# Filter rows in halves, later k-v products and paired value tiles in a fused attention and long-convolution kernel

## The chip, the cores and the metric

The kernel runs on one core of one Trainium2 chip. Its time is the device time of one execution in microseconds. The core has five engines that run their own instruction streams and wait for one another through semaphores: TensorE (PE, with the weight loads shown as PEld), VectorE (DVE), ScalarE (ACT), GpSimd (POOL) and SyncE (SP). SP, ACT and POOL issue DMA transfers, which run on 16 DMA engines.

## The reference

Two independent branches are computed in bf16 and laid side by side in the output (2048 x 1024).

- A: attention over x (2048 x 512) with 32 heads of width 16. `qkv = x @ wqkv`, softmax of `q k^T / 4` over all 2048 keys (no mask), times v, heads joined, `@ wo`.
- B: a gated long convolution over 512 channels. k is shifted and weighted by four taps, `kv = k_shift * v`, then every channel d is convolved causally with its own filter `ssm_k[d]` of length 2048 (the reference does it by FFT), `kv * ssm_D` is added, and the result is multiplied by q.

## The kernel before

*Attention.* Scores are made transposed, in blocks of 128 keys x 512 queries of one head: four query blocks, eight groups of four heads, 16 key tiles, 2048 blocks. The blocks are walked in 695 steps (`chunks`), of three blocks each, or of two in every second step of the first 56 (`N_EARLY`) and at the end. In a step PE makes the scores (L453) into one of two sets of three PSUM banks, ACT takes the exponential of the whole set in one instruction (L460), and two steps later PE multiplies by V (L525). Of each group, four blocks have their exponential computed on DVE instead (L478 to L494). Since the scores use two bank sets, PE can be one step ahead of ACT.

*Convolution.* Channel d's filter is written reversed and zero-padded to a scratch in HBM (`kz_scratch`); loading it with a step of one element from partition to partition gives a 128 x 2048 Toeplitz row `WR[:, r, :]`, 512 KB. There are 12 places r for such rows. Places 5 to 9 first hold k turned (`KTR`), from which the product of k and v is made, so they come free only when a block of 128 channels (c = 0 to 3) has its four products. A quad `qd` is four channels; its convolution is 16 lags of four small matmuls each (`conv_lags`, L648). Lag n uses columns 128 (15 - n) to 128 (16 - n) of the row, so lags 0 to 7 read the second half of a row and lags 8 to 15 the first. Two quads share PSUM bank 7, after which DVE evicts (L662); after eight quads a turn, a product with q and, after eight turns, stores follow.

*Order.* The instruction lists of all engines are written by one loop over the steps T: scores, products with V, then `emit_bg`, which puts at most one piece of background work into the step. The background jobs are the projections of q, k and v (L285, L292, L299), the products of k and v (`prod_job`, L341, evicted at L353), the output projection (L594) and the convolution. Each job has a due step and an earliest step in `todo`; a job is cut into pieces of about half a PSUM bank's matmuls. Before step 56 jobs use bank 5, later bank 7. `st["time"]` is a budget: each step adds 0.42, 0.74 or 0.78 and each piece takes 0.47. The lags are spread evenly up to step `CONV_END`, at most five a step.

*Loads.* `load_wr` issues filter rows on SP, in the order of the channels, as soon as a place is named free; SP waits for the last matmul of the row that was there. SP's queue is in order, so a load that waits holds all that follow, the loads of q and the stores of B among them. `land` is the planner's own estimate of when a row will be there, 1.33 us a row; `conv_ready` lets lags be placed only from that step on. On the chip PE waits for the real load, and the scores that follow wait behind it in PE's queue. Three other queues are touched by the change: DVE's pieces `kv_pieces` (copies of q's weights, turning of the filter), the filler matmuls `warm`, and `keep_busy_end`.

Of the kernel before, what the change touches and what calls it, by code (L numbers as in the profile page):

```python
# [37 lines left out]
CONV_END = 668  # L38
# [57 lines left out]
def bass_concat_heads__mha_block__ssm_conv_h3__prompt_kernel(  # L96
# [89 lines left out]
    d_wr = [DmaSem(sem(f"d_wr{i}")) for i in range(R_W)]  # L186
# [34 lines left out]
    h_w0 = dve.op(lambda e: e.memset(PT[:, 0, 0:512], 0.0))  # L221
# [55 lines left out]
    def pe_unit(u, bank, dcs=(0, 1, 2, 3)):  # L277
# [9 lines left out]
        elif kind == "k":  # L287
# [6 lines left out]
        else:  # L294
            _, kt, z = u
            deps += h_x[kt // 4] + [h_wv]

            def mm(e, dc):
                return e.matmul(PS[:, bank, 0:256], lhsT=xT[:, dc, kt * 128:(kt + 1) * 128],  # L299
                                rhs=WV[:, dc, 256 * z:256 * z + 256], start=(dc == 0), stop=(dc == 3))  # L300

# [7 lines left out]
    def evac_unit(u, bank, h, eng=None):  # L309
        kind = u[0]  # L310
        if kind == "q":
            _, qb, g = u
            hh = dve.op(lambda e: e.tensor_scalar(QT[:, qb % 2, g, :], PS[:, bank, :], QSCALE, None, ALU.mult),  # L313
                        [h])
            h_q[(qb, g)] = hh
        elif kind == "k":
# [7 lines left out]
        else:  # L324
            _, kt, z = u
            dst = VAF[:, kt, 0:H * VW].rearrange("p (h e) -> p h e", e=VW)[:, 16 * z:16 * z + 16, 0:DH]
            src = PS[:, bank, 0:256].rearrange("p (h e) -> p h e", h=16)
            hh = dve.op(lambda e: e.tensor_copy(dst, src), [h, h_vaf1])  # L328
            h_v[(kt, z)] = hh
        bank_free[bank] = hh  # L330

# [44 lines left out]
    def warm(e):  # L376
        ins = None
        for _ in range(12):
            ins = e.matmul(PS[:, 0, :], lhsT=PT[:, 0, 0:128], rhs=PT[:, 0, 0:512], start=True, stop=True)
        return ins  # L380
    pe.op(warm, [h_w0])
# [161 lines left out]
    def finish_group(n, h, T):  # L543
# [8 lines left out]
        assert n < 4 or len(h_prod) == 16  # L552
# [145 lines left out]
    def unit_job(*u):  # L698
        def job(T, bank):
            if u[0] == "v":  # L700
                return [lambda: unit(u, bank)]
# [3 lines left out]
    def prod_job(c, j):  # L705
        def job(T, bank):
            def last():
                prod_out(c, j, bank, prod_mm(c, j, 2, 4, bank))
                if sum(k[0] == c for k in h_prod) == 4:
                    slots.extend((r, h_prod_mm[c]) for r in ((5,), (6,), (7,), (8, 9))[c])  # L710
# [23 lines left out]
    todo = [(when(0, 0, kt) + 1, x_at[kt // 4], 1, unit_job("v", kt, 0)) for kt in range(KT)]  # L734
    todo += [(when(0, 4, kt) + 1, 0, 1, unit_job("v", kt, 1)) for kt in range(KT)]
    todo += [(when(0, 2 * o, 4 * sc), x_at[sc], 2, unit_job("k", o, sc)) for o in range(4) for sc in range(4) if o or sc]
# [205 lines left out]
```

## Time and profile before

| | |
|---|---|
| median of 3 runs | 925.04 us (923.96 to 927.89) |
| the profiled execution | 928.67 us |
| its span | 926.7 us |
| granted TensorE clock, mean | 0.987 |
| ACT busy | 892.0 us, 96% |
| PE busy | 771.5 us, 83% |
| DVE busy | 637.7 us, 69% |
| DMA moved | 289.36 MB, mean 312 GB/s |

The span goes from the first to the last instruction; the time of the execution has some 2 us around it. A busy share is an average over all stages. In a group of instructions, `128x1536` is partitions by elements, the number after `x` the count; the idle time in front of a group has the name of the engine and line that ended it. In the windows, a row gives the stretch, its length, the busy time of PE, PEld, DVE, ACT and POOL with their instructions, the clock, the share of the DMA engines and GB/s. In the DMA rows, "under 512 B" and so on count packets by size. The code numbers the steps from 0; the exponential of step T is the T-th row of L460.

### The profile page before, as it was taken

The page shows a single profiled execution, that of the slowest core. Times are in us where ns is not written, and L with a number is a line of the kernel's source. Part 1 is how long each engine was busy: PE and PEld are TensorE (multiplying, and loading weights), DVE is VectorE, ACT ScalarE, POOL GpSimd, SP SyncE. Part 2 cuts the span into 40 slices and gives each one's busy share as a digit, 9 for nine tenths or more (in the row PEclk, how much of TensorE's full clock was granted, in tenths as well). Part 3 has the DMA queues.
Part 4 walks back from the last instruction along what each step waited for, and adds up shares of the span by engine and source line. Part 5 has one row for each costly group of instructions (what it writes and reads, how often), then busy time and mean ns, then how long its engine had stood idle before and what let it go on. Part 6 is the DMA issues. An engine that isn't in the chain of part 4 may idle for free.

```text
span 926.7 us, 29497 instructions
## 1 busy us (share of the span) xinstructions
PE 771.5 (83%) x13428; PEld 354.6 (38%) x13482; DVE 637.7 (69%) x817; ACT 892.0 (96%) x701; POOL 22.2 (2%) x38
## 2 busy tenths in 40 slices
PE   7998888888788878888888788888888888877887
PEld 2333433333334333334334334333334443444422
DVE  3426678778677676777777767686777777667674
ACT  4999999999999999999999989999999999999997
POOL 3000000003000000000000000000000000000000
PEclk8999999999999999999999989999999999999999
DMA  9970741889999999999999999999999999999810
GB/s 246 257 253 31 242 139 46 318 294 296 405 370 371 353 370 337 374 326 379 378 373 378 346 391 364 335 379 364 386 382 379 328 364 356 403 397 376 334 47 23
DMA packets 105035, 289.36 MB, mean 312 GB/s; under 512 B 25680, under 2 KB 38480, under 8 KB 104528
## 3 DMA queue, kind: packets, MB, share of 16 engines
q1 hardware_dynamic: 101680, 284.33, 84.8%
q8 instruction: 106, 1.74, 0.7%
q0 software_dynamic: 832, 2.10, 0.7%
q10 hardware_dynamic: 2400, 1.05, 0.5%
q14 instruction: 17, 0.14, 0.0%
HBM read 277.35 MB, written 6.42 MB: 306 GB/s over the span
## 4 chain that ended last, share of the span: by engine, by line
ACT 69%; PE 15%; DVE 8%; DMA 5%; issue 1%; SPq 1%; ACTq 0%; POOL 0%; DVEq 0%
ACT PT L460 69%; PE PS L453 4%; DMA WR<-kz_scratch 4%; PE PS L525 4%; DVE EH L489 2%; PE PS L341 2%; PE PS L299 2%; PE PS L594 2%; PE PS L292 1%; PE PS L648 1%; DVE KV L353 1%; DVE KTo L322 1%; DMA SHK<-in_B_shift_k_dram 1%; SPq L173 1%; DVE PTD L494 1%
## 5 line engine op out<-in xcount | busy, mean ns | idle before, releaser
L460 ACT ACTIVATE PT<-PS 128x1536 bf16<-128x1536 f32 (+1 forms) x695 | 888.0, 1572 | 21.4 <-PE PS L453 20.6
L453 PE MATMUL PS<-QT,KTo 32*128 32x512 bf16 x2048 | 275.0, 389 | 105.9 <-ACT PT L460 94.0
L648 PE MATMUL PS<-WR,KV 128*11 128x128 bf16 (+15 forms) x8192 | 295.2, 224 | 18.5 <-DMA WR<-kz_scratch 9.2
L525 PE MATMUL PS<-PT,VAF 128*32 128x512 bf16 x1928 | 292.4, 393 | 1.3 <-DVE VAF L328 1.0
L648 PEld LDWEIGHTS PS<-WR,KV 128*9 128x9 bf16 (+15 forms) x8192 | 191.9, 107 | 61.1 <-issue 41.3
L453 PEld LDWEIGHTS PS<-QT,KTo 32*128 32x128 bf16 x2048 | 67.7, 91 | 257.7 <-ACT PT L460 210.5
L489 DVE SCALAR_TENSOR_TENSOR EH<-EH,EM 128x1024 f32<-128x1024 f32 x120 | 151.7, 1264 | 3.4
L478 DVE TENSOR_SCALAR EI<-PS 128x512 int32<-128x512 f32 x120 | 85.0, 708 | 72.1 <-PE PS L453 70.7
L525 PEld LDWEIGHTS PS<-PT,VAF 128*32 128x32 bf16 x1928 | 69.0, 93 | 148.1 <-issue 138.8
L489 DVE SCALAR_TENSOR_TENSOR EH<-EM 128x1024 f32<-128x1024 f32 x60 | 77.2, 1287 | 0.0
L494 DVE SCALAR_TENSOR_TENSOR PTD<-EH,EI 128x1024 bf16<-128x1024 f32 x60 | 74.5, 1241 | 1.7
L546 DVE STREAM_TRANSPOSE DT<-PS 128x512 f32<-128x512 f32 x31 | 22.9, 739 | 60.0 <-PE PS L525 57.0
L662 DVE CAST YB<-PS 128x256 bf16<-128x256 f32 x64 | 26.8, 419 | 27.5 <-PE PS L525 13.8
L482 DVE TENSOR_SCALAR EM<-EI 128x1024 int32<-128x1024 int32 x60 | 44.4, 739 | 1.7
L484 DVE TENSOR_SCALAR EI<-EI 128x1024 int32<-128x1024 int32 x60 | 42.8, 714 | 2.1
L313 DVE TENSOR_SCALAR QT<-PS 128x512 bf16<-128x512 f32 x32 | 22.1, 690 | 26.1 <-PE PS L285 26.1
L285 PE MATMUL PS<-xT,WQP 128*128 128x512 bf16 x101 | 32.3, 382 | 6.5 <-issue 3.0
L594 PE MATMUL PS<-WKV,OTN 128*128 128x512 bf16 x114 | 33.2, 382 | 4.4 <-issue 1.6
L525 PE MATMUL PS<-PTD,VAF 128*32 128x512 bf16 x120 | 24.0, 397 | 1.3 <-DVE PTD L494 1.2
L773 PE MATMUL PS<-IDN,ZR 128*16 128x128 bf16 x308 | 24.8, 222 | 0.2 <-issue 0.2
L328 DVE CAST VAF<-PS 128x256 bf16<-128x256 f32 x32 | 13.5, 421 | 16.3 <-PE PS L299 16.2
L563 DVE STREAM_TRANSPOSE OTN<-OB 128x512 bf16<-128x512 bf16 (+1 forms) x33 | 23.7, 717 | 0.7
(61 smaller groups left out, 252.9 us busy)
## 6 DMA issues: line engine op xcount, KB each, us to landing
WR<-kz_scratch SPq DMA_DIRECT2D x512, 512.0 KB, 7.9
kz_scratch<-WR SPq DMA_DIRECT2D x1, 2176.0 KB, 12.6
QN<-in_B_q_dram SPq DMA_DIRECT2D x8, 256.0 KB, 8.8
out_dram<-KV SPq DMA_DIRECT2D x16, 128.0 KB, 2.9
out_dram<-OUTA POOLq DMA_DIRECT2D x12, 128.0 KB, 5.2
QT<-in_B_ssm_k_dram SPq DMA_DIRECT2D x1, 1024.0 KB, 5.6
QN<-in_B_ssm_k_dram SPq DMA_DIRECT2D x1, 1024.0 KB, 7.6
OTN<-in_B_v_dram SPq DMA_DIRECT2D x1, 1024.0 KB, 6.5
```

Source lines behind the costliest of these rows:

```text
L285: return e.matmul(PS[:, bank, :], lhsT=WQP[:, dc, g, :], rhs=xT[:, dc, qb * 512:(qb + 1) * 512], start=(dc == 0), stop=(dc == 3))
L453: ins = e.matmul(PS[:, bank, :], lhsT=KTo[32 * s:32 * s + 32, g // 2, kt * 128:(kt + 1) * 128], rhs=QT[32 * s:32 * s + 32, qb % 2, g, :], ...
L460: h_exp[T] = act.op(lambda e: e.activation(PT[:, T % R_PT, 0:n * QB], PS[:, banks[0]:banks[0] + n, :].rearrange("p b f -> p (b f)"), ACT.E ...
L478: h_fix[i] = dve.op(lambda e: e.tensor_scalar(EI[:, i % 2, :], PS[:, bank, :], FIX_LO, FIX_ADD, ALU.max, ALU.add), [h, h_pair.get(p - 1)])
L482: st["m"] = dve.op(lambda e: e.tensor_scalar(EM[:, :, :], EI[:, :, :], 0x7fffff, 0x3f800000, ALU.bitwise_and, ALU.bitwise_or), [h_fix[i], ...
L484: st["e"] = dve.op(lambda e: e.tensor_scalar(EI[:, :, :], EI[:, :, :], 0x7f800000, 0x40000000, ALU.bitwise_and, ALU.bitwise_xor), [st["m"]])
L489: st["h"] = dve.op(lambda e: e.scalar_tensor_tensor(EH[:, :, :], src, (B3, B2, B1)[j], m, ALU.add, ALU.mult), [st["m"], st.get("h")])
L494: lambda e: e.scalar_tensor_tensor(PTD[:, :, :], EH[:, :, :], B0, EI[:, :, :].bitcast(FP32), ALU.add, ALU.mult), [st["h"], st["e"], h_ptd. ...
L525: ins = e.matmul(PS[32 * s:32 * s + 32, pvb(qb * NG + g), :], lhsT=VAF[:, kt, h * VW:h * VW + 32], rhs=rhs, start=(kt == 0), stop=(kt == K ...
L594: ins = e.matmul(PS[:, bank, :], lhsT=OTN[:, oslot(qb * NG + g), t * 128:(t + 1) * 128], rhs=WOP[:, g, :], start=(g == 0), stop=(g == NG - 1))
L648: ins = e.matmul(PS[32 * c:32 * c + NB - n, BGB, col:col + 128], lhsT=KV[:, n:NB, d], rhs=WR[:, slot_of[d], 128 * (NB - 1 - n):128 * (NB - ...
L662: bank_free[BGB] = h_yb[qd // 8] = dve.op(lambda e: e.tensor_copy(dst, src), [h, h_turn.get(qd // 8 - 1)])
```

## The change

- Each filter row is loaded as two halves of 256 KB, with a place and a semaphore of its own for each (24 in all). The second half (z = 1) is loaded ahead of the first for four rows at a time. A half's place is free again after the last lag that reads it. Lags 0 to 7 wait for the second halves alone. The planner books 0.67 us a half.
- The products of k and v for channel block 0 are due at steps 50 to 53 (before 40 to 43). Those of blocks 1 to 3 are due at 88 to 152, mixed, where they were due at 54 to 87. The places they hold come free accordingly.
- The value projections are made in pairs of key tiles: two tiles' matmuls go into one bank and one DVE instruction evicts both. Only the first two tiles stay single.
- In the first 56 steps the budget adds 0.45 a step and a piece takes 0.55. Projections of k and q are due four steps earlier; q of the second query block is allowed from step 140 or 156 (before 92).
- DVE's `kv_pieces` run in steps 4 to 6 and after 10 (before 0 to 2 and after 10). Three filler matmuls are added in step 0.
- `CONV_END` is 674 (before 668); the end filler is left out in steps in which bank 7 was evicted.

```diff
-CONV_END = 668
+CONV_END = 674
...
-    d_wr = [DmaSem(sem(f"d_wr{i}")) for i in range(R_W)]
+    d_wr = [DmaSem(sem(f"d_wr{i}")) for i in range(2 * R_W)]
...
+    def v_mm(kt, z, i, bank):
+        def fn(e):
+            ins = None
+            for dc in range(4):
+                ins = e.matmul(PS[:, bank, 256 * i:256 * i + 256], lhsT=xT[:, dc, (kt + i) * 128:(kt + i + 1) * 128],
+                               rhs=WV[:, dc, 256 * z:256 * z + 256], start=(dc == 0), stop=(dc == 3))
+            return ins
+        return pe.op(fn, h_x[kt // 4] + [h_wv, bank_free[bank] if i == 0 else None])
+
+    def v_out(kt, z, n, bank, h):
+        dst = VAF[:, kt:kt + n, 0:H * VW].rearrange("p t (h e) -> p t h e", e=VW)[:, :, 16 * z:16 * z + 16, 0:DH]
+        src = PS[:, bank, 0:256 * n].rearrange("p (t h e) -> p t h e", t=n, e=DH)
+        bank_free[bank] = hh = dve.op(lambda e: e.tensor_copy(dst, src), [h, h_vaf1])
...
-    pe.op(warm, [h_w0])
+    pe.op(lambda e: warm(e, 12, 0), [h_w0])
...
-    slots = [(r, None) for r in (0, 1, 2, 3, 4, 10, 11)]
+    slots = {z: [(r, None) for r in (0, 1, 2, 3, 4, 10, 11)] for z in range(2)}
     slot_of, land = {}, {}
+    next_row = [0, 0]
     def load_wr(T):
-        while slots and len(slot_of) < C:
-            d = len(slot_of)
-            r, h = slots.pop(0)
-            src = bass.AP(tensor=kz_ap.tensor, offset=kz_ap[d, 0].offset, ap=[[1, 128], [1, S]])
-            h_wr[d] = dma(sp, d_wr[r], WR[:, r, :], src, [h_kzw[0], h])
-            slot_of[d] = r
-            st["dma"] = max(st["dma"], now(T) + 2.5) + 1.33
-            land[d] = st["dma"] + 1.0
+        while True:
+            z = 1 if next_row[1] // 4 == next_row[0] // 4 and next_row[1] % 4 >= next_row[0] % 4 and next_row[0] % 4 == 0 else 0
+            d = next_row[z]
+            if d == C or not slots[z]:
+                return
+            next_row[z] += 1
+            r, h = slots[z].pop(0)
+            src = bass.AP(tensor=kz_ap.tensor, offset=kz_ap[d, 1024 * z].offset, ap=[[1, 128], [1, 1024]])
+            h_wr[(d, z)] = dma(sp, d_wr[2 * r + z], WR[:, r, 1024 * z:1024 * z + 1024], src, [h_kzw[0], h])
+            slot_of[(d, z)] = r
+            st["dma"] = max(st["dma"], now(T) + 2.5) + 0.67
+            land[(d, z)] = st["dma"] + 1.0
...
-        deps = [h_wr[4 * qd + c] for c in range(4)] + [h_prod[(4 * qd // 128, j)] for j in range(4)]
+        deps = [h_wr[(4 * qd + c, z)] for c in range(4) for z in ([1] if n0 < 8 else []) + ([0] if n1 > 8 else [])] + [h_prod[(4 * qd // 128, j)] for j in range(4)]
...
-                                   rhs=WR[:, slot_of[d], 128 * (NB - 1 - n):128 * (NB - n)],
+                                   rhs=WR[:, slot_of[(d, 1 - n // 8)], 128 * (NB - 1 - n):128 * (NB - n)],
...
         h = pe.op(fn, deps)
+        for z in range(2):
+            if n0 < (NB, 8)[z] <= n1:
+                slots[z].extend((slot_of[(4 * qd + c, z)], h) for c in range(4))
+        load_wr(T)
         if n1 == NB:
-            slots.extend((slot_of[4 * qd + c], h) for c in range(4))
-            load_wr(T)
...
-    todo = [(when(0, 0, kt) + 1, x_at[kt // 4], 1, unit_job("v", kt, 0)) for kt in range(KT)]
-    todo += [(when(0, 4, kt) + 1, 0, 1, unit_job("v", kt, 1)) for kt in range(KT)]
+    todo = [(when(0, 0, kt) + 1, x_at[kt // 4], n, unit_job("v", kt, 0, n)) for kt, n in [(0, 1), (1, 1)] + [(i, 2) for i in range(2, KT, 2)]]
+    todo += [(when(0, 4, kt) + 1, 0, 2, unit_job("v", kt, 1, 2)) for kt in range(0, KT, 2)]
...
-    todo += [((40, 54, 70, 84)[c] + j, max(18 + 2 * c, 24 if j >= 2 else 0), 2, prod_job(c, j))
+    todo += [(((50, 51, 52, 53), (88, 100, 106, 112), (94, 118, 124, 146), (100, 134, 140, 152))[c][j], max(18 + 2 * c, 24 if j >= 2 else 0), 2, prod_job(c, j))
              for c in range(4) for j in range(4)]
...
-        return (T >= N_EARLY and d < C and land.get(d + 3, 1e9) <= now(T)
+        return (T >= N_EARLY and d < C and land.get((d + 3, 1 - st["lag"] // 8), 1e9) <= now(T)
...
             unit(("q", 0, 1), 5)
+            pe.op(lambda e: warm(e, 3, 7), [bank_free[7]])
...
-        st["time"] = min(st["time"] + (0.78 if T >= N_EARLY else 0.42 if T % 2 else 0.74), 1.1)
+        st["time"] = min(st["time"] + (0.78 if T >= N_EARLY else 0.45), 1.1)
...
-                st["time"] -= 0.47
+                st["time"] -= 0.47 if T >= N_EARLY else 0.55
...
+            if n0 < 8 < n1 and land.get((4 * st["qd"] + 3, 0), 1e9) > now(T):
+                n1 = 8
...
-        elif st["qd"] == C // 4 and T < NT - 14:
+        elif st["qd"] == C // 4 and T < NT - 14 and bank_free[BGB] is st["seen"]:
             keep_busy_end(T)
...
-        if kv_pieces and (T < 3 or T > 10):
+        if kv_pieces and (4 <= T < 7 or T > 10):
```

More of the change, by code (lines that the diff above doesn't have):

```diff
@@ L312, in evac_unit @@
             _, qb, g = u
+            assert qb != 1 or all((c, 2 + g // 4) in h_prod for c in range(4))
             hh = dve.op(lambda e: e.tensor_scalar(QT[:, qb % 2, g, :], PS[:, bank, :], QSCALE, None, ALU.mult),
@@ L323, in evac_unit @@
             h_k[(o, sc)] = hh
[L324 to L329, printed above, removed]
-        bank_free[bank] = hh
+        bank_free[bank] = hh
+    def v_mm(kt, z, i, bank):
[10 more added lines that the diff above has]
+        bank_free[bank] = hh = dve.op(lambda e: e.tensor_copy(dst, src), [h, h_vaf1])
+        for i in range(n):
+            h_v[(kt + i, z)] = hh
     def unit(u, bank, eng=None):
@@ L550, in finish_group @@
         ob = OB[:, :].rearrange("p (b i) -> p b i", i=32)
-        assert n < 4 or len(h_prod) == 16
+        assert not 4 <= n < 12 or all((c, n // 4 - 1) in h_prod for c in range(4))
         def scale():
@@ L787, in emit_bg, with bg_step @@
     def emit_bg(T):
+        bg_step(T)
+        st["seen"] = bank_free[BGB]
+    def bg_step(T):
         if not st["wop"] and len(h_v) == 2 * KT and len(h_k) == 16:
@@ L807, in emit_bg @@
             jobs = bg_jobs(T)
-            if jobs and (st["gap"] or not conv_ready(T) or urgent(T, jobs)):
+            if jobs and (st["gap"] or T >= N_EARLY and not conv_ready(T) or urgent(T, jobs)):
                 j = jobs[0]
```

31 lines of the change are left out of this document (14 added, 17 removed).

## The prediction

> **What bounds the kernel now.** I read the page's engine totals first, then the ACT waits, then ACT's stages in windows, then the DMA rows.
>
> ```profile
> span 926.7 us, 29497 instructions
> PE 771.5 (83%) x13428; PEld 354.6 (38%) x13482; DVE 637.7 (69%) x817; ACT 892.0 (96%) x701; POOL 22.2 (2%) x38
> L460 ACT ACTIVATE PT<-PS 128x1536 bf16<-128x1536 f32 (+1 forms) x695 | 888.0, 1572 | 21.4 <-PE PS L453 20.6
> 24.00:86.00 62.00, 58.27 (x494) 24.60 (x498) 24.18 (x44) 57.28 (x50) 0.00 (x0) 1.00 0.67 198
> 86.00:161.00 75.00, 64.57 (x810) 27.81 (x817) 58.44 (x83) 71.84 (x56) 0.00 (x0) 1.00 0.40 134
> ```
>
> ScalarE is the bound: 695 exponentials fill 888.0 of 926.7 us, and the change leaves all 695 (the same blocks, the same 120 on VectorE). Only ACT's holes can move. Its holes between exponentials are 20.6 us, nearly all waits for the scores matmul. In the last two rows (columns: window, length, busy time of PE, PEld, DVE, ACT, POOL, clock, DMA share, GB/s) ACT lacks 62.00 - 57.28 = 4.7 us and 75.00 - 71.84 = 3.2 us, with PE at 94% and 86%.
>
> ```profile
> 15.98 1.02 ACT L460 ACTIVATE PT<-PS 128x1024 bf16<-128x1024 f32 x1 [0.99 <-PE PS L453]
> 18.04 1.45 ACT L460 ACTIVATE PT<-PS 128x1536 bf16<-128x1536 f32 x1 [1.03 <-PE PS L453]
> ...
> 22.14 2.37 ACT L460 ACTIVATE PT<-PS 128x1536 bf16<-128x1536 f32 x2 [1.03 <-PE PS L453]
> ...
> 44.42 2.41 ACT L460 ACTIVATE PT<-PS 128x1536 bf16<-128x1536 f32 x2 [0.18 <-PE PS L453]
> 47.01 2.37 ACT L460 ACTIVATE PT<-PS 128x1536 bf16<-128x1536 f32 x2 [0.18 <-PE PS L453]
> ...
> 52.22 4.74 ACT L460 ACTIVATE PT<-PS 128x1536 bf16<-128x1536 f32 x4 [0.23 <-PE PS L453]
> ...
> 241.50 2.80 ACT L460 ACTIVATE PT<-PS 128x1536 bf16<-128x1536 f32 x2 [1.21 <-PE PS L453]
> ...
> 535.51 1.47 ACT L460 ACTIVATE PT<-PS 128x1536 bf16<-128x1536 f32 x1 [2.25 <-PE PS L453]
> ```
>
> Three kinds of hole are seen. At 16 to 22 us steps lose about 1 us each. Around 45 us a pair of steps takes 47.01 - 44.42 = 2.59 us where two pairs without a hole (52.22) take 4.74, 2.37 each: about 0.2 us a pair. At 241 and 535 single holes of 1.21 and 2.25 us stand beside late filter rows.
>
> The second resource is the DMA stream of filter rows, 512 loads of 512 KB:
>
> ```profile
> WR<-kz_scratch SPq DMA_DIRECT2D x512, 512.0 KB, 7.9
> L173 SPq DMA_DIRECT2D WR<-kz_scratch x512: 319/434/2493, 50.0 to 869.5; - x171
> PE PS L648 <- DMA WR<-kz_scratch: 9.2, 12, 2.4
> SPq L173 <- PE PS L648: 435.3, 90, 30.9
> DMA packets 70420, 243.14 MB, mean 367 GB/s; under 512 B 7754, under 2 KB 11850, under 8 KB 70322
> q1 hardware_dynamic: 69490, 239.53, 97.2%
> ```
>
> (The last two are for 208 to 870 us.) The stream runs at 367 GB/s with the 16 engines 97% occupied, and the convolution on PE waited for it 9.2 us in 12 places. It is just not the bound.
>
> **The change part by part.** Durations are of the profiled execution, 928.67 us around its span; the three runs' median is 925.04, so the sum is scaled by 0.9961.
>
> 1. *First steps, to 24 us.*
>
> ```profile
> 11.45 0.69 DVE L313 TENSOR_SCALAR QT<-PS 128x512 bf16<-128x512 f32 x1 [0.89 <-PE PS L285]
> 12.06 1.97 DVE L250 COPY WQP<-OTN 128x256 bf16<-128x256 bf16 x2
> 13.95 0.41 DVE L328 CAST VAF<-PS 128x256 bf16<-128x256 f32 x1
> 12.20 0.39 PE L453 MATMUL PS<-QT,KTo 32*128 32x512 bf16 x2 [0.79 <-DVE QT L313]
> 1.22 4.58 PE L379 MATMUL PS<-PT 128*128 128x512 bf16 x12 [1.22 <-DVE PT L221]
> 10.00:20.00 10.00, 8.20 (x45) 2.75 (x45) 5.29 (x12) 6.29 (x5) 3.95 (x4) 0.76 0.98 294
> ```
>
> The WQP copies (1.97 us for two) stood ahead of the first value eviction; they move behind step 4, so that eviction can go about 0.8 us earlier and with it the first product with V. Three added filler matmuls cost 3 x 4.58/12 = 1.15 us of PE, of which 0.79 lies in the wait ahead of the second scores matmul; 0.4 us may stick out. Against that they may save some of the half clock (0.76 granted in 10 to 20 us). The holes are 0.99 + 1.03 + 1.03 and two smaller. Bounds +0.4 and -4; taken -2.0, since half of it hangs on the clock.
>
> 2. *Fewer pieces, 24 to 86 us.* The order of the two built programs gives, from step 20 to 55, 37 background pieces before and 26 after (22 of the 37 were half products; 8 stay), and 12 against 8 from step 8 to 19.
>
> ```profile
> 46.02 0.62 PE L341 MATMUL PS<-OUTA,WR 128*128 128x128 bf16 x8
> 46.57 0.39 PE L453 MATMUL PS<-QT,KTo 32*128 32x512 bf16 x3
> 46.90 0.40 PE L525 MATMUL PS<-PT,VAF 128*32 128x512 bf16 x3
> ```
>
> From piece to piece is 1.2 to 1.4 us on PE, over ACT's 2.37/2 = 1.19. Fifteen pieces at 0.6 us free 9 us of PE where ACT lacks 4.7. Where two jobs still stand back to back a hole of 0.1 a step stays. Bounds 0 and -4.7; taken -4.2. Making values in pairs leaves PE's matmuls as they are; it turns VectorE evictions of 0.41 us into half as many wider ones, on an engine busy 24.18 of 62 us: nothing.
>
> 3. *What is moved later, 86 to 208 us.* From step 56 to 149 the pieces go from 49 to 66, the convolution lags from 192 to 116. Before, 3.2 us of hole came with some 38 pieces up to step 111, 0.09 each; 17 more pieces are +1.5, less 0.3 for fewer evictions on VectorE. Bounds -3.2 (DVE was the cause) and +3.9 (0.23 each). Taken +1.2. Late products keep five filter places shut until step 104 to 143; DMA share is 0.40 there, so the stream has room, but the lags must be made up later (4).
>
> 4. *Rows in halves.* The conv's first eight lags need only the second half of four rows; the other half may come about 8 lags, two steps or 2.6 us, later. The waits at 241 (1.21) and 535 (2.25, with the slow PE after it) are of that size. Bounds 0 and -4.5; taken -3.2. SP issues 512 more loads at 434 ns, 222 us, and it waits 435 us for places: covered; an issue blocked behind a place not yet free holds the later ones as now.
>
> The price is in the packets: 2 KB instead of 4 KB. No row has 2 KB, so I bound it from a stretch of 512 B rows and one of filter rows alone (61 to 65 us, 230 to 250 us; the third row gives the length of a step, the fourth the landing of a store):
>
> ```profile
> DMA packets 2105, 1.27 MB, mean 317 GB/s; under 512 B 76, under 2 KB 2042, under 8 KB 2104
> ...
> DMA packets 2229, 8.14 MB, mean 407 GB/s; under 512 B 248, under 2 KB 248, under 8 KB 2226
> ...
> L460 ACT ACTIVATE PT<-PS x695: 1017/1603/2032, 10.5 to 918.3; 128x1536 bf16<-128x1536 f32 x142, 128x1024 bf16<-128x1024 f32 x32
> out_dram<-KV SPq DMA_DIRECT2D x16, 128.0 KB, 2.9
> ```
>
> At full occupation a packet of 600 B costs an engine 16 x 600/317 = 30 ns, one of 4096 B with its share of signals 16 x 4096/407 = 161 ns. The line between them gives 2048 B 85 ns: 16 x 2048/85 = 386 GB/s, 5% less. Bounds 407 and 317; I take 386, nearest to the 4 KB row on that line. Need: from step 148 on 948 of 1024 halves (248.5 MB) are still to be issued, by step 664, 516 steps of (918.3 - 10.5)/694 = 1.308 us = 675 us, with 7 MB of other traffic (243 less 237 above): 378 GB/s. So it just fits in the mean. It doesn't at the end: at step 600 136 halves are left, 35.7 MB or 92.4 us at 386, and about 7.9 us are queued; the last is wanted at about step 676, 99.6 us later: 0.7 us short, and with each landing behind the planner's clock, +1 to +9. Taken +3.0.
>
> The Trainium skill, Perfetto Trace Analysis, DMA Optimizations, says that small DMAs carry much overhead and names merging 2 KB into 4 KB as the cure of a DMA-bound kernel; this change does the reverse. The Trainium skill, DMA: Bandwidth & Descriptors, Why small descriptors are slow, puts about 3 cycles on a packet, 67/64 against 131/128 beats: 2.3% by an estimate from that page. By it the end term would be about +1.5 and not +3.0; the two rows above speak for 5%, and none has this size.
>
> 5. *The end.* By the order the convolution's last lags stand at step 677 instead of 667, with 17 steps, 22 us, left for the last turn and stores that land 2.9 us after issue: nothing, unless the convolution is later than that. Its pace (the new CONV_END) and the test before end fillers change only where lags and fillers stand.
>
> Sum: -2.0 - 4.2 + 1.2 - 3.2 + 3.0 = -5.2, 923.5 of 928.67; scaled, **919.8 us**. Below 0.5%, 4.6 us, two kernels can hardly be told apart here, so the gain is near that bound.
>
> **Rivals.**
>
> *The filter stream becomes the bound (slower).* It needs 378 GB/s. If the 367 GB/s of the whole stretch, and not the 407 of a backlog, is all that 4 KB packets give, 2 KB ones give 0.95 x 367 = 349. Half way to 386, at 367, the 255.5 MB take 696 us where the steps allow 675. Of these 21 us the lead in the places covers some 8 (at step 600 888 halves are issued and 864 used up, 16 us of stream, 7.9 of them queued): +13 instead of +3, 930; at 349 it is 732 us, +49, 966. It decides from about 378 GB/s down. For it: 97.2% occupation. Against: 407 GB/s as soon as a backlog stands.
>
> The Trainium skill's rule on small DMAs (Perfetto Trace Analysis, above) is this rival.
>
> *The end gives all back (no change).* The opening gains 5 but the last 75 steps have a late half in every second step; PE idles as after 529 us:
>
> ```profile
> 529.00:534.00 5.00, 2.75 (x63) 1.34 (x60) 4.51 (x9) 4.26 (x4) 0.00 (x0) 1.00 1.03 385
> 534.00:541.00 7.00, 6.41 (x88) 2.92 (x90) 3.69 (x4) 5.17 (x4) 0.00 (x0) 0.51 1.05 404
> ```
>
> PE 55% busy for 5 us was followed by a clock of 0.51, in which ACT lost 1.8 of 7 us. Two or three of these with +5 for late halves make the end +8: 924 to 926. For it: no slack in the sum of (4). Against: waits under about 0.5 us are covered by the lead of one chunk in PSUM.
>
> *The moved pieces only move their holes.* If PE's holes come with the piece wherever it stands, (2) is -3 and (3) +3: 921 to 925; part of the case above.
>
> **How the numbers follow.** Gain as summed: 0.48. Near no change, by the end or by the moved pieces: 0.27. The stream as the bound: 0.25. Low end 911: (1), (2) and (4) at their bounds and the end at +1 are -4 - 4.7 - 4.5 + 1.2 + 1 = -11, 914, and 3 more with (3) on its good side. High end 936: inside the slower rival, whose part above it holds about 0.12. The likeliest case alone reaches from 912 to 921.
>
> **What will show it.** Right: ACT's hole in 24 to 86 us under 1.5 us; no hole over 1 us at 241 and 535; GB/s in stretches with a backlog 380 to 390. Wrong: convolution waits for filter rows well over 9.2 us, in a train after about 790 us; a backlog rate under 370; clock under 0.9 after 800 us; ACT's hole in 86 to 161 us over 5 us.

## The result and the profile after

The changed kernel takes 929.62 us (median of 20 runs, 927.04 to 932.29) where the kernel before takes 925.02 us (20 runs, 920.21 to 931.33): a ratio of 1.0042, interval 1.0024 to 1.0060. It is 0.4% slower, inside the 0.5% below which I had called two kernels hardly distinguishable, but with an interval that leaves out 1: a gain of 0.5% was forecast and a loss of 0.4% came. The time is 9.8 us above the forecast of 919.8; it lies in the range of 911 to 936 only because that range had been drawn wide enough for the slower rival.

The page after, its totals, the exponentials and the filter loads:

```profile
span 925.4 us, 29882 instructions
PE 767.1 (83%) x13245; PEld 350.4 (38%) x13299; DVE 634.5 (69%) x802; ACT 891.9 (96%) x701; POOL 22.0 (2%) x38
...
L463 ACT ACTIVATE PT<-PS 128x1536 bf16<-128x1536 f32 (+1 forms) x695 | 887.9, 1540 | 20.3 <-PE PS L456 19.3
...
WR<-kz_scratch SPq DMA_DIRECT2D x1024, 256.0 KB, 8.2
```

ACT's work is the same, 887.9 us, and its idle time even falls a little, from 21.4 to 20.3 us. That hides the result: the profiled execution after (927.15 us) lies near the lowest of its kernel, the one before (928.67 us) 3.6 us above its median, so these two executions differ by -1.5 us where the medians differ by +4.6. What can be read is where the holes stand. The windows after (length, busy PE, PEld, DVE, ACT, POOL, clock, DMA share, GB/s):

```profile
10.00:20.00 10.00, 9.31 (x64) 3.36 (x62) 3.45 (x11) 8.97 (x8) 4.03 (x4) 1.00 0.99 298
...
24.00:76.00 52.00, 47.36 (x375) 17.41 (x380) 17.93 (x31) 51.17 (x47) 0.00 (x0) 1.00 0.82 229
76.00:150.00 74.00, 63.81 (x704) 26.96 (x710) 57.86 (x76) 70.12 (x55) 0.00 (x0) 1.00 0.19 62
150.00:205.00 55.00, 46.82 (x670) 20.20 (x667) 41.79 (x50) 50.96 (x40) 8.13 (x9) 0.94 0.64 196
...
790.00:890.00 100.00, 79.35 (x1682) 39.16 (x1682) 62.51 (x75) 92.89 (x71) 0.00 (x0) 0.95 1.05 384
```

The same view of the kernel before, for two stretches that the prediction didn't show:

```profile
161.00:205.00 44.00, 36.45 (x706) 17.07 (x709) 33.09 (x42) 44.00 (x35) 0.00 (x0) 1.00 0.84 297
...
790.00:890.00 100.00, 81.32 (x1783) 42.43 (x1784) 66.01 (x81) 97.07 (x77) 0.00 (x0) 0.95 0.88 343
```

The opening is better: ACT is busy 8.97 of the 10 us from 10 to 20 us, and lacks 0.8 us from 24 to 76 us. Then it turns. From 150 to 205 us ACT lacks 4.0 us, where before it lacked nothing from 161 to 205 us, and from 790 to 890 us it lacks 7.1 us against 2.9. Before, the DMA engines moved 297 GB/s ahead of 205 us (161 to 205); after, 196 (150 to 205). PE's waits for filter rows, first of the whole kernel after, then of the stretch from 780 to 890 us, after and before:

```profile
PE PS L656 <- DMA WR<-kz_scratch: 21.1, 30, 1.9
...
PE PS L656 <- DMA WR<-kz_scratch: 18.2, 26, 1.9
```

```profile
PE PS L648 <- DMA WR<-kz_scratch: 3.7, 6, 1.4
```

They went from 9.2 to 21.1 us, and 18.2 us of it are one train at the end. The exponentials in that train, with the idle time ahead of each in brackets:

```profile
807.18 1.45 ACT L463 ACTIVATE PT<-PS 128x1536 bf16<-128x1536 f32 x1 [1.84 <-PE PS L456]
...
819.38 11.05 ACT L463 ACTIVATE PT<-PS 128x1024 bf16<-128x1024 f32 x8 [1.14 <-PE PS L456]
...
872.28 1.46 ACT L463 ACTIVATE PT<-PS 128x1536 bf16<-128x1536 f32 x1 [1.31 <-PE PS L456]
```

The DMA rows after, for 230 to 250 us and for 208 to 889 us (with its main queue):

```profile
DMA packets 4207, 7.69 MB, mean 384 GB/s; under 512 B 468, under 2 KB 468, under 8 KB 4205
...
DMA packets 141351, 253.60 MB, mean 372 GB/s; under 512 B 15541, under 2 KB 19637, under 8 KB 141245
q1 hardware_dynamic: 140669, 250.43, 102.2%
```

Halves of 2 KB packets flow at 384 GB/s where whole rows gave 407, and the 16 engines are occupied from 208 us to the end of the convolution. The start of the same exponential in both profiles gives the balance by stage:

| step | before, us | after, us | change within the stage |
|---|---|---|---|
| 8 | 24.7 | 20.4 | -4.3 |
| 56 | 85.8 | 75.7 | -5.8 |
| 150 | 210.3 | 205.3 | +5.1 |
| 600 | 795.6 | 787.8 | -2.8 |
| 694 | 918.3 | 916.9 | +6.4 |

Ten microseconds are won up to step 56. Then 5.1 are lost up to step 150 and 6.4 in the last 94 steps; the stage between them keeps 2.8.

One hole is new and large, at 198 us. DVE, PE, ACT and POOL there, after:

```profile
190.84 3.51 POOL L582 MEMSET WKV<- 128x4096 bf16 x1 [176.74 <-PE PS L528]
192.09 2.81 DVE L485 TENSOR_SCALAR EM<-EI 128x1024 int32<-128x1024 int32 x1
...
195.54 0.68 DVE L356 TENSOR_TENSOR KV<-PS,QT 128x512 bf16<-128x512 f32 x1
...
196.68 0.63 PE L285 MATMUL PS<-xT,WQP 128*128 128x512 bf16 x1 [3.30 <-DVE KV L356]
...
197.91 1.45 ACT L463 ACTIVATE PT<-PS 128x1536 bf16<-128x1536 f32 x1 [3.21 <-PE PS L456]
```

POOL clears the place of the output weights (L582) from 190.84 to 194.35 us. DVE's integer step at 192.09 (L485, 0.77 us in the mean of the page) takes 2.81 us and ends 0.55 us behind the clearing; the eviction of a product of k and v (L356), which now falls here, waits behind it, PE's q projection waits for that bank, and the scores wait behind the projection. Before, the same two instructions met too. No hole followed there, and no eviction of a product stood behind them:

```profile
210.94 3.78 POOL L579 MEMSET WKV<- 128x4096 bf16 x1 [196.99 <-PE PS L525]
...
213.21 2.07 DVE L482 TENSOR_SCALAR EM<-EI 128x1024 int32<-128x1024 int32 x1
```

The Trainium skill, SBUF — State Buffer, Who interferes with whom, describes the pair of SBUF ports that DVE and GpSimd share as an exclusive lock: a DVE instruction in a mode that uses both ports and a GpSimd instruction wait for the whole of one another. Both rows fit: DVE ended 0.55 and 0.56 us after the clearing. Which mode L485 ran in is not in the rows.

**Theories.** S: from 208 us on the stream of filter rows is the limit in the end, so what is lost in bytes by then (late products) and in rate (2 KB packets) comes back as time, and what the opening wins is taken back. L: the loss is local, the hole at 198 us and the late holes that PE makes by itself; the halves are harmless.

### The profile page after: what moved, and what is told of

Its sections match the earlier page's. It is cut to its first block, busy times and chain, and to the rows that moved or that the text cites. A ratio compares the mean times of both kernels' runs of the same rounds, so it can differ in the third digit from the quotient of the medians.

```text
span 925.4 us, 29882 instructions
## 1 busy us (share of the span) xinstructions
PE 767.1 (83%) x13245; PEld 350.4 (38%) x13299; DVE 634.5 (69%) x802; ACT 891.9 (96%) x701; POOL 22.0 (2%) x38
## 4 chain that ended last, share of the span: by engine, by line
ACT 66%; PE 16%; DMA 8%; DVE 6%; SPq 2%; issue 1%; ACTq 0%; DVEq 0%
ACT PT L463 66%; DMA WR<-kz_scratch 8%; PE PS L456 4%; PE PS L528 4%; SPq L173 2%; PE PS L323 2%; PE PS L597 2%; PE PS L656 1%; PE PS L344 1%; DVE EH L492 1%; PE PS L292 1%; DVE VAF L331 1%; PE PS L285 1%; DVE KTo L315 1%; DVE KV L356 1%
## 5 line engine op out<-in xcount | busy, mean ns | idle before, releaser
L463 ACT ACTIVATE PT<-PS 128x1536 bf16<-128x1536 f32 (+1 forms) x695 | 887.9, 1540 | 20.3 <-PE PS L456 19.3
L656 PE MATMUL PS<-WR,KV 128*2 128x128 bf16 (+15 forms) x8192 | 287.8, 224 | 34.3 <-DMA WR<-kz_scratch 21.1
L656 PEld LDWEIGHTS PS<-WR,KV 128*5 128x5 bf16 (+15 forms) x8192 | 187.9, 107 | 83.3 <-issue 63.0
L481 DVE TENSOR_SCALAR EI<-PS 128x512 int32<-128x512 f32 x120 | 84.9, 708 | 73.9 <-PE PS L456 72.4
L485 DVE TENSOR_SCALAR EM<-EI 128x1024 int32<-128x1024 int32 x60 | 46.2, 771 | 1.5
L306 DVE TENSOR_SCALAR QT<-PS 128x512 bf16<-128x512 f32 x32 | 22.1, 690 | 30.6 <-PE PS L285 30.6
L331 DVE CAST VAF<-PS 128x512 bf16<-128x512 f32 (+1 forms) x17 | 11.2, 659 | 21.7 <-PE PS L323 21.7
L323 PE MATMUL PS<-WKV,xT 128*128 128x256 bf16 x128 | 19.5, 275 | 3.2 <-DVE KV L356 1.3
```

The source lines that it names most:

```text
L323: ins = e.matmul(PS[:, bank, 256 * i:256 * i + 256], lhsT=xT[:, dc, (kt + i) * 128:(kt + i + 1) * 128], rhs=WV[:, dc, 256 * z:256 * z + 25 ...
L463: h_exp[T] = act.op(lambda e: e.activation(PT[:, T % R_PT, 0:n * QB], PS[:, banks[0]:banks[0] + n, :].rearrange("p b f -> p (b f)"), ACT.E ...
L481: h_fix[i] = dve.op(lambda e: e.tensor_scalar(EI[:, i % 2, :], PS[:, bank, :], FIX_LO, FIX_ADD, ALU.max, ALU.add), [h, h_pair.get(p - 1)])
L485: st["m"] = dve.op(lambda e: e.tensor_scalar(EM[:, :, :], EI[:, :, :], 0x7fffff, 0x3f800000, ALU.bitwise_and, ALU.bitwise_or), [h_fix[i], ...
L656: ins = e.matmul(PS[32 * c:32 * c + NB - n, BGB, col:col + 128], lhsT=KV[:, n:NB, d], rhs=WR[:, slot_of[(d, 1 - n // 8)], 128 * (NB - 1 - ...
```

## The experiments

Every ratio is to the kernel before, run on the same chip. e1 to e4 ran on one chip; a comparison with the changed kernel goes through two such ratios.

### The four parts apart: e1_rows, e2_early, e3_halves, e4_opening

e1_rows is the changed kernel with whole rows: `load_wr`, the places, the lags' waits and `conv_ready` as before.

```diff
...
-            src = bass.AP(tensor=kz_ap.tensor, offset=kz_ap[d, 1024 * z].offset, ap=[[1, 128], [1, 1024]])
-            h_wr[(d, z)] = dma(sp, d_wr[2 * r + z], WR[:, r, 1024 * z:1024 * z + 1024], src, [h_kzw[0], h])
+            src = bass.AP(tensor=kz_ap.tensor, offset=kz_ap[d, 0].offset, ap=[[1, 128], [1, S]])
+            h_wr[d] = dma(sp, d_wr[r], WR[:, r, :], src, [h_kzw[0], h])
...
```

> The changed kernel with whole rows of 4 KB packets again (one place, one semaphore a row), all else as changed, the late products too. Theory S, the stream: 2 KB packets run at 386 GB/s, and with 249 MB still to come at 205 us that is what ends the convolution; with whole rows the backlog rate is 405 to 410 GB/s again, the waits of the convolution for rows fall from 21 us to under 10, and the time to 918 to 924. Theory L, the late products: their own holes (3.2 us at 198 us, and the 9 MB less loaded by then) cost the time, the packets nothing: 928 to 931.

e2_early is the changed kernel with the products due as before:

```diff
-    todo += [(((50, 51, 52, 53), (88, 100, 106, 112), (94, 118, 124, 146), (100, 134, 140, 152))[c][j], max(18 + 2 * c, 24 if j >= 2 else 0), 2, prod_job(c, j))
+    todo += [((40, 54, 70, 84)[c] + j, max(18 + 2 * c, 24 if j >= 2 else 0), 2, prod_job(c, j))
```

> The changed kernel with the products of k and v due where they were before (40 to 87), halves kept. Theory S: rate still 386 GB/s, but by the order 46 rows and not 38 are issued by step 148, 4.2 MB or 11 us of stream: half of the late waits go, 922 to 927. Theory L: all of the loss goes, 916 to 920, and the hole of 3.2 us near 198 us with it.

e3_halves is the kernel before with the halves alone (e1's edit, the other way round).

> The kernel before with halves of rows alone (places, semaphores, waits); the order of all other work stays. Theory S: backlog rate 386 in place of 407 GB/s, 248 MB from 208 us on take 642 us of 661, so the waits of the convolution for rows rise from 9 to 12 to 20 us, mostly after 790 us, and the time to 927 to 932. Theory L: 924 to 926, or less by the waits at 241 and 535 us that halves spare.

e4_opening is the changed kernel with both undone: the opening and the pairs of values remain, and with them the new `CONV_END`, the test before end fillers and the later q. What the table calls the opening is all of these.

> The changed kernel with both undone, whole rows and products due at 40 to 87: what is left is the opening with fewer pieces, value pairs, fillers and the later copies. Both theories: the opening's gain of 8 to 10 us at step 56 is kept in part; theory S says 912 to 918, the best of the four, and theory L the same as the second, 916 to 920. If the gain is lost here too, neither is the cause: 924 and more.

| kernel | opening | rows | products | median, us | ratio |
|---|---|---|---|---|---|
| before | old | whole | early | 924.61 | 1 |
| e3_halves | old | halves | early | 929.45 | 1.0054 (1.0027 to 1.0081) |
| e4_opening | new | whole | early | 920.21 | 0.9951 (0.9929 to 0.9974) |
| e2_early | new | halves | early | 925.48 | 1.0008 (0.9982 to 1.0033) |
| e1_rows | new | whole | late | 925.77 | 1.0001 (0.9975 to 1.0028) |
| changed | new | halves | late | 929.62 | 1.0042 (1.0024 to 1.0060) |

By the ratios, at 924.6 us: the opening alone is worth -0.49%, -4.5 us. The halves cost 0.54% on the kernel before, 0.57% on e4 (to e2) and 0.41% on e1 (to the changed kernel): 3.8 to 5.3 us. The late products cost 0.50% (e4 to e1) and 0.34% (e2 to the changed kernel): 3.1 to 4.6 us. By the intervals each of these costs is known to some 3 us. The parts add up nearly: the two losses outweigh the gain. In the times, S's numbers held for e2 and e3, and e1 fell between S and L; e4 is a little slower than both had it, so the opening's 10 us of the profiles are not all there. L failed on e2: its largest hole near 198 us is 0.46 us, and it still takes 925.5 us.

In the waits S did less well. It asked for waits under 10 us and 405 to 410 GB/s in e1, and for waits of 12 to 20 us in e3. The waits for filter rows in e1's profile and in e3's, and e1's stream from 230 to 250 us, are these:

```profile
PE PS L651 <- DMA WR<-kz_scratch: 14.8, 16, 3.8
```

```profile
PE PS L653 <- DMA WR<-kz_scratch: 9.1, 11, 2.3
```

```profile
DMA packets 2071, 7.53 MB, mean 377 GB/s; under 512 B 238, under 2 KB 238, under 8 KB 2069
```

e1's whole rows reached 377 GB/s there, in engines that were 99% occupied and not 103% as before. e3 waited 9.1 us, no more than the kernel before (9.2, in an execution 3.6 us above its median), and yet was 5 us slower. So the sum of the waits in one profile does not rank these kernels; that the halves cost time is shown by the ratios, and the way from the rate to the time is plain only in the changed kernel, e6, e8 and e9.

The granted clock goes with the times: averaged over the executions it is 0.993 in e4, 0.991 in the kernel before beside it, 0.988 to 0.990 in e1, e2 and e3, and 0.986 in the changed kernel. Within the kernel before, executions of 0.998 and 0.982 took 920.9 and 931.1 us. So a part of each loss may be a lower clock; whether the clock falls because PE waits, as the prediction's rows after 529 us suggest, no run separates.

What the late products take from the stream is seen in what was issued up to 205 us. The filter loads in that stretch of the changed kernel, of e1_rows, e4_opening and before, in this order, each from its own trace:

```profile
WR<-kz_scratch SPq DMA_DIRECT2D x77, 256.0 KB, 6.0
```

```profile
WR<-kz_scratch SPq DMA_DIRECT2D x39, 512.0 KB, 6.9
```

```profile
WR<-kz_scratch SPq DMA_DIRECT2D x48, 512.0 KB, 7.5
```

```profile
WR<-kz_scratch SPq DMA_DIRECT2D x56, 512.0 KB, 6.5
```

77 halves are 38.5 rows: with late products, whole or halved, 9 rows fewer are under way than in e4, 4.7 MB, which is 12 us of a stream at 386 GB/s. e4 itself has 8 fewer than before. From step 56 to 148 its trace has 572 matmuls of the convolution and 128 of products, where the trace before has 768 and 80: there too, pieces that the opening no longer does stand in the place of lags.

### One transfer more, or packets half as long: e6_two_cols, e9_one_2k, e7_two_parts

All three are the kernel before with nothing changed but the shape of a row's transfer. e6_two_cols loads each row as two transfers of half the columns, under one place and one semaphore:

```diff
-            src = bass.AP(tensor=kz_ap.tensor, offset=kz_ap[d, 0].offset, ap=[[1, 128], [1, S]])
-            h_wr[d] = dma(sp, d_wr[r], WR[:, r, :], src, [h_kzw[0], h])
+            for z in (1, 0):
+                src = bass.AP(tensor=kz_ap.tensor, offset=kz_ap[d, 1024 * z].offset, ap=[[1, 128], [1, 1024]])
+                h_wr[d] = dma(sp, d_wr[r], WR[:, r, 1024 * z:1024 * z + 1024], src, [h_kzw[0], h])
```

> The kernel before with each filter row loaded by two transfers of half its columns, 2 KB packets, into one place and with one semaphore; nothing else is changed, and no wait is for a half. Packet size as the cost: backlog rate 386 GB/s, 928 to 931, as with halves that have places of their own, or 1 to 2 us more, since no wait is shortened. If the cost lies in places, order or waits of halves: 924 to 926.

934.63 us, ratio 1.0109 (1.0065 to 1.0152), some 2 us above the most that was expected. Its stream from 230 to 250 us, and the convolution's waits:

```profile
DMA packets 4201, 7.68 MB, mean 384 GB/s; under 512 B 467, under 2 KB 467, under 8 KB 4198
```

```profile
PE PS L649 <- DMA WR<-kz_scratch: 21.0, 17, 4.4
```

e9_one_2k separates packets from transfers: one transfer a row, with the two halves in turned order inside it, so that the packets are 2 KB long.

```diff
-            src = bass.AP(tensor=kz_ap.tensor, offset=kz_ap[d, 0].offset, ap=[[1, 128], [1, S]])
+            src = bass.AP(tensor=kz_ap.tensor, offset=kz_ap[d, 1024].offset, ap=[[1, 128], [-1024, 2], [1, 1024]])
+            dst = WR[:, r, 1024:S]
+            dst = bass.AP(tensor=dst.tensor, offset=dst.offset, ap=[dst.ap[0], [-1024, 2], [1, 1024]])
-            h_wr[d] = dma(sp, d_wr[r], WR[:, r, :], src, [h_kzw[0], h])
+            h_wr[d] = dma(sp, d_wr[r], dst, src, [h_kzw[0], h])
```

> The kernel before with one transfer and one semaphore a row as before, but the row's two column halves in turned order inside the transfer, so that every packet is 2 KB. If packet size is the cost, backlog rate 386 GB/s and 930 to 935, as with two transfers of column halves (934.6). If the number of transfers was the cost there, 924 to 926 and a rate over 400.

934.93 us, ratio 1.0115 (1.0073 to 1.0157), the same as e6. The same two views:

```profile
DMA packets 3996, 7.73 MB, mean 387 GB/s; under 512 B 234, under 2 KB 234, under 8 KB 3994
```

```profile
PE PS L650 <- DMA WR<-kz_scratch: 26.4, 29, 3.4
```

So the number of transfers makes no difference that these runs can see; the packets cost about 10 us (1.1% of 924.6), and the kernel before has not that much room in its stream. Against this the own places and waits of the halves earn back about 5 us (e3's 1.0054 in place of 1.0109 or 1.0115, with intervals that overlap a little). On these numbers the idea of the halves works, and its packets cost twice what it brings.

e7_two_parts was meant as the other control, two transfers with 4 KB packets, by cutting a row into two times 64 partitions:

```diff
-            src = bass.AP(tensor=kz_ap.tensor, offset=kz_ap[d, 0].offset, ap=[[1, 128], [1, S]])
-            h_wr[d] = dma(sp, d_wr[r], WR[:, r, :], src, [h_kzw[0], h])
+            for z in range(2):
+                src = bass.AP(tensor=kz_ap.tensor, offset=kz_ap[d, 64 * z].offset, ap=[[1, 64], [1, S]])
+                h_wr[d] = dma(sp, d_wr[r], WR[64 * z:64 * z + 64, r, :], src, [h_kzw[0], h])
```

> The kernel before with each filter row loaded by two transfers of 64 partitions each: as many transfers as with halves, but packets of 4 KB. Packet size as the cost: backlog rate 405 to 410 GB/s and 924 to 926, no change. If the number of transfers costs (SP's issues, signals, short transfers): 928 to 931, as in the run with two column halves.

1152.89 us (1113.27 to 1182.20), 25% longer; its executions also had a lower clock (0.868 in the profiled one). The stream from 300 to 700 us, with its main queue:

```profile
DMA packets 38081, 113.27 MB, mean 283 GB/s; under 512 B 6978, under 2 KB 11074, under 8 KB 38034
...
q1 hardware_dynamic: 37746, 111.77, 101.4%
```

The engines are fully occupied at 283 GB/s with long packets. Since two transfers a row do no harm in e6, what is left is that each spans 64 partitions. The run says nothing on its question; e9 answers it.

### Fewer rows, and the hole at 198 us: e5_fewer, e8_memset

e5_fewer is the changed kernel without the rows of every 16th quad:

```diff
-            h_wr[(d, z)] = dma(sp, d_wr[2 * r + z], WR[:, r, 1024 * z:1024 * z + 1024], src, [h_kzw[0], h])
+            if d // 4 % 16 == 15:
+                h_wr[(d, z)] = None
+            else:
+                h_wr[(d, z)] = dma(sp, d_wr[2 * r + z], WR[:, r, 1024 * z:1024 * z + 1024], src, [h_kzw[0], h])
```

> The changed kernel with the filter rows of every sixteenth quad not loaded (8 of 128 quads, 16.8 MB; those quads multiply what their places held, so B's output is wrong in 32 channels); the order of all work stays. If the stream is what ends the kernel, 16.8 MB at 386 GB/s are 43 us of it: the waits of the convolution for rows fall from 21 us to under 5, and the time by 4 to 8, to 921 to 926, where the hole at 198 us and the opening are left. If places, semaphores or the late products' own holes cost the time, it stays at 928 to 931.

926.11 us, ratio 1.0005 (0.9980 to 1.0030): 3.4 us under the changed kernel by the ratios, with intervals that overlap, and at the edge of what S had. The convolution waited 12.1 us, not under 5, so the run supports S in direction only.

What S means at the end can be read in bytes. These were moved from step 600 to the end of the convolution in the changed kernel (787.8 to 896 us), and before (795.6 to 880 us):

```profile
DMA packets 21765, 39.86 MB, mean 368 GB/s; under 512 B 2425, under 2 KB 2425, under 8 KB 21747
```

```profile
DMA packets 8730, 31.92 MB, mean 378 GB/s; under 512 B 978, under 2 KB 978, under 8 KB 8716
```

At the measured 384 GB/s the 39.86 MB take 104 us. The 76 steps from 600 to 676, where they are used up, take 99 us at 1.308 us a step: the stream is 4 to 5 us late, and the stage came out 6.4 us longer. Before, 31.92 MB at 407 GB/s take 78 us of the 88 that 67 steps take. For e5 the same sum (35.71 MB) gives 93 us, some room; why it still waited stays open.

e8_memset is the changed kernel with POOL's clearing in eight pieces, so that DVE can come in between:

```diff
-        h = pool.op(lambda e: e.memset(WOP, 0.0), [h_last])
+        for i in range(8):
+            h = pool.op(lambda e, i=i: e.memset(WOP[:, i, :], 0.0), [h_last])
```

> The changed kernel with GpSimd's clearing of the output weights (L582, one instruction of 3.5 us) cut into eight. If the hole of 3.2 us at 198 us is VectorE held up behind that one instruction, its EM at 192 us falls from 2.8 us to about 1, the hole to under 1 us, and the time by 1 to 3 us, less what the stream takes back: 926 to 929. If the hole comes from the late products themselves, it stays, and so does the time, 929 to 931.

929.63 us, ratio 1.0056 (1.0029 to 1.0084): no gain. Its timeline at the place, and the convolution's waits:

```profile
191.48 4.87 POOL L583 MEMSET WKV<- 128x512 bf16 x8 [178.22 <-PE PS L528]
192.72 0.76 DVE L485 TENSOR_SCALAR EM<-EI 128x1024 int32<-128x1024 int32 x1
...
196.11 14.46 ACT L463 ACTIVATE PT<-PS 128x1536 bf16<-128x1536 f32 x11 [0.78 <-PE PS L456]
```

```profile
PE PS L657 <- DMA WR<-kz_scratch: 20.7, 25, 2.1
```

DVE's step is back at 0.76 us, the hole went from 3.21 to 0.78 us, and step 150 came at 202.7 us in place of 205.3. The time did not change: the waits stayed at 20.7 us, and the gain was gone at once. Six steps later PE and then ACT sit idle:

```profile
211.80 0.63 PE L657 MATMUL PS<-WR,KV 128*10 128x128 bf16 x16 [3.01 <-issue]
```

```profile
213.02 1.45 ACT L463 ACTIVATE PT<-PS 128x1536 bf16<-128x1536 f32 x1 [2.45 <-PE PS L456]
```

The view names no releaser (`issue`), but by the semaphore events of the trace a filter half landed at 211.74 us, just ahead of that matmul. The same half landed at 211.54 us in the changed kernel, though e8 had issued it 3.3 us earlier (200.23 for 203.51). This is the plainest run against L: the largest hole of the profile is worth nothing in the changed kernel, because the rows are no earlier for it.

### Held places or displaced lags: e11_places

The late products do two things: they displace lags of the convolution, and they keep the places 5 to 9 shut for longer. e11_places is e4 with only the second:

```diff
-                    slots.extend((r, h_prod_mm[c]) for r in ((5,), (6,), (7,), (8, 9))[c])
+                    later.append(((45, 105, 139, 143)[c], lambda: slots.extend((r, h_prod_mm[c]) for r in ((5,), (6,), (7,), (8, 9))[c])))
```

> The opening alone again, with the five places under the turned k named free only at the steps of the changed kernel (45, 105, 139, 143); the pieces stand as in the opening alone. If the late products cost by the places they hold, 923 to 926. If they cost by their pieces, which push convolution lags behind step 148 (by the order 38 rows are issued by then, here 44 as in the opening alone), 919 to 922.

922.60 us, ratio 0.9977 (0.9954 to 1.0000): 2.4 us over e4, with intervals that just overlap, and between the two expectations. It issues 47 rows up to 205 us, one fewer than e4, so most of the 9 rows that are missing with late products are missing because lags that would empty places stand later. How the cost of 3.1 to 4.6 us is shared between the two stays open.

### A faster kernel: e10_best

e10_best is e4 with the clearing in pieces and two bursts taken out of SP's queue: the four loads of q for the second half of the channels stand eight steps apart instead of in one step, and the eight stores of the first half of B go out every sixth step instead of every second.

```diff
+        for i in range(8):
+            h = pool.op(lambda e, i=i: e.memset(WOP[:, i, :], 0.0), [h_last])
...
-                        load_qn(1, [hh])
+                        for t in range(0, NB, 4):
+                            later.append((T + 2 + 2 * t, lambda t=t: load_qn(1, [hh], t)))
...
-                        later.append((T + 1 + t, lambda i=i, t=t: store_y(i, t, hh)))
+                        later.append((T + 1 + (1 if i else 3) * t, lambda i=i, t=t: store_y(i, t, hh)))
```

> The opening alone (whole rows, products due at 40 to 87) with GpSimd's clearing in eight pieces, and the loads of q and the stores of B around step 397 spread over some 45 steps in place of 15. If the stream has slack there as the theory says (whole rows, 44 rows issued by step 148), the hole of 2.5 us at 542 us goes with its half clock: 916 to 919. If what is gained before is taken back later, as when the clearing was cut in the changed kernel, 919 to 921.

916.64 us, ratio 0.9904 (0.9870 to 0.9939), 1% under the kernel before. The window from 500 to 600 us in e4 and then in e10, with the exponential behind the largest hole of that stretch:

```profile
500.00:600.00 100.00, 82.76 (x1527) 38.11 (x1527) 71.33 (x87) 96.75 (x76) 2.16 (x4) 0.97 1.00 367
...
541.91 1.47 ACT L463 ACTIVATE PT<-PS 128x1536 bf16<-128x1536 f32 x1 [2.45 <-PE PS L456]
```

```profile
500.00:600.00 100.00, 82.80 (x1594) 39.17 (x1599) 74.40 (x89) 99.14 (x78) 2.16 (x4) 1.00 1.00 381
...
542.39 18.24 ACT L463 ACTIVATE PT<-PS 128x1536 bf16<-128x1536 f32 x14 [0.53 <-PE PS L456]
```

The convolution's waits for filter rows over the whole kernel, in the same order:

```profile
PE PS L651 <- DMA WR<-kz_scratch: 11.7, 13, 3.1
```

```profile
PE PS L652 <- DMA WR<-kz_scratch: 6.7, 11, 1.9
```

The hole of 2.45 us at 542 us is down to 0.53, the clock stays at 1.00 there, and the waits fall by 5 us. SP's queue ahead of the hole, in e4 and then in e10, shows what stood in front of the rows:

```profile
521.37 5.63 SPq L173 DMA_DIRECT2D QN<-in_B_q_dram  x4
527.04 2.91 SPq L173 DMA_DIRECT2D out_dram<-KV  x2
```

```profile
522.46 0.44 SPq L173 DMA_DIRECT2D out_dram<-KV  x1
522.94 0.47 SPq L173 DMA_DIRECT2D QN<-in_B_q_dram  x1
```

In e4 no filter row is issued from 521.37 to 529.99 us; in e10 the next rows follow at 526.36. The edits were not run apart, so how the 3.6 us between e4 and e10 divide is open; the clearing stands 350 us ahead of this hole. The halves were to remove this hole (step 4 of the prediction); e10 is nearly rid of it with 4 KB packets.

## Why the prediction was wrong, step by step

The step that failed is (4), rows in halves: it priced the 2 KB packets at +3.0 us, and they cost about 10. Beside it, (3) priced the late products at +1.2 us, and they cost 3.1 to 4.6. With the measured sizes, going from before by e4 and e2 to the changed kernel, the sum is -4.5 (opening) + 5.3 (halves) + 3.1 (late products) = +3.9 us, 0.4%, where -6.2 - 0.2 + 1.2 = -5.2 had been forecast.

- *First steps (1), -2.0: right in size.* The profiles give -4.3 to step 8, but the profiled execution before had a clock of 0.76 from 10 to 20 us. e3, which has the old opening, kept the full clock, as its window shows, and reached step 8 at 22.1 us, against 20.4 after: -1.7. So the low clock on which half of the term hung does not come in every execution of that opening.

```profile
10.00:20.00 10.00, 7.79 (x54) 2.96 (x55) 5.23 (x12) 7.87 (x8) 4.03 (x4) 1.00 0.98 299
```

- *Fewer pieces (2), -4.2: right where it stands, not at the end.* ACT's hole from 24 to 76 us is 0.8 us, under the 1.5 named. The steps 8 to 56 are 5.8 us shorter, more than the bound of -4.7, which had counted ACT's holes alone. Of the -6.2 of both steps e4 kept 4.5 us; that the rest was given back later fits the traces and is not shown by a run of its own.
- *What is moved later (3), +1.2: the term failed, too small.* It counted holes between 86 and 208 us and set the displaced lags down to (4) at no price of their own. The "room" that it saw in a DMA share of 0.40 could not be used: with the places shut the share from 76 to 150 us fell to 0.19. The stage cost 5.1 us in the profile, 3.2 of it a collision of POOL and DVE that I had not looked for. But e8 and e2 show that the hole isn't the price. What is left is the 9 rows that start later; e11 did not settle how much of it they are. Measured over the whole kernel: 3.1 to 4.6 us.
- *Rows in halves (4), -3.2 and +3.0: the rate was right, and the price worked out from it failed.* 386 GB/s was forecast and 384 measured. The waits spared come to about 5 us by e3 against e6 and e9. The packets cost about 10 us by e9, not 3.0, because I charged them at the end alone, where the last rows came out 0.7 us short, and took the rest of the stream to have room in the mean (378 of 386 GB/s). e9's profile is 8.9 us longer than the one before between steps 150 and 694, of which 5.2 us lie between 150 and 400 and only 2.4 after 600: a stream that fits in the mean already makes single rows late. And I let the opening's microseconds count in full on top, although every step that ACT reaches earlier leaves such a stream less time for the same row.
- *The end (5), nothing:* nothing in the runs speaks against it.
- *What was to show it.* There is no hole over 1 us at 241 us, but one of 1.55 us at 567; the backlog rate is in the 380 to 390 named. Of the signs named for "wrong" one came, convolution waits well over 9.2 us in a train after about 790 us: 18.2 us. The others did not; the clock from 790 to 890 us is 0.95.
- *The rivals.* The stream as the bound was the mechanism, but not by the rate of 367 that the rival asked for, nor at its price of 930 to 966 us. It decided at the full 384, because the last 39.86 MB need 104 us and the steps leave 99. "The end gives all back" (924 to 926) came nearest: it put the end at +8, and the last 94 steps lost 6.4 us, in a train of late halves as it said. It was 3.6 us short, about what (3) lacked in the profile (5.1 for 1.2). The moved pieces did not just move their holes: from 76 to 150 us ACT lacks 3.9 us, where it lacked 3.2 from 86 to 161.

The Trainium skill's rule on small DMAs (Perfetto Trace Analysis, DMA Optimizations), which the prediction weighed as a rival, was borne out if "DMA" is read as packet: in e9 the transfer is still 512 KB, its packets are 2 KB instead of 4 KB, and that took 5% of the rate (407 to 387) and 10 us. The estimate of 2.3%, and of +1.5 us from it, was too low.

## What to carry to other kernels

When a stream is occupied nearly all the time (97% here), read its slack as bytes still wanted by a step against bytes it can bring by then, at several steps and not only in the mean; any work that starts it later, and any gain ahead of it, is booked there. Be wary of cutting a load into parts with their own places where the packets get shorter: here they cost twice what the places brought. Before a stream is made finer, look for bursts of other transfers in its queue: in the faster kernel here, spreading them stood in for the halves.

## What the runs showed of the hardware that was not expected

- Transfers of 64 partitions with 4 KB packets brought 283 GB/s at full occupation where 128 partitions brought 407 (e7). The Trainium skill, SBUF — State Buffer, "Can I just issue two DMAs to hit both halves?", says that only one transfer over all 128 partitions reaches all 16 ports; the run agrees in direction.
- The kernel takes the same time with a row as two transfers or as one, if the packets are alike (e6 and e9, 934.63 and 934.93 us, each known to some 4 us).
- One clearing of 3.51 us on POOL, which only writes, stretched an integer instruction on DVE to 2.81 us, where it took 0.76 with the clearing in eight pieces (e8 against the changed kernel). DVE's instruction just before, which reads PSUM, took 0.65 us beside the same clearing, no more than its usual 0.7 (L481).
